# A planned order of 1300 steps, planned again with TensorE's instruction fetches and two corrected durations

## The chip, the cores and the metric

The kernel runs on one core of a Trainium2 chip. The metric is the device time of one execution in microseconds (us). All operands are float32 at the kernel's interface; the products are formed from two or three float32r (rounded float32) parts, so that the result has float32 accuracy.

## The reference, cut to what matters

Three layers follow each other on a batch of 2 with 768 positions: an attention with a local window and block summaries (8 heads of 64), a token-mixing layer with a rotation, and a gated layer with a second mixing of tokens.

```python
# attention: q, k, v (2, 8, 768, 64)
k_sum, v_sum = max and mean of k, v over blocks of 32 positions
scores = [scale*q@k.T where |i-j| < 16, else -1e9 ; scale*q@k_sum.T + log(32)]
x = softmax(scores) @ [v ; v_sum]                # heads joined: (2, 768, 512)
# token mixing
theta = x @ w_theta
y = w_tok_r @ (x*cos(theta)) + w_tok_i @ (x*sin(theta))
u = x + y
x = u + max(u @ w_ch, 0)
# gated layer
h = gelu(x @ w_in);  u, v = halves of h
v = layernorm(v) * g_ln;  v = w_sg @ v + b_sg
out = x + (u*v) @ w_out
```

## The kernel before, in words

**The steps.** The kernel function (L547) does not write instructions where they stand in the text. It calls `op(...)` (L391) some 1300 times. Each call names a step, the engines that may do it with an estimated duration on each, the steps that it comes after, the buffers that it takes, and, for a load, its size. Examples are `S` (L915: 52 small matmuls, the scores of one pair of heads and one half of the positions), `PT` (L944: three transposes), `O` (L960: 24 small matmuls with the values), `X` (L981: three transposes), `th` (L1019: three matmuls of 512 columns for theta), `y` (L1098: six matmuls of the token mixing), `ch`, `iv`, `iu` (twelve matmuls of 512 columns each), `Qp` (L1435: nine of 384 columns) and `o` (L1490: the output).

**The planner.** `Order.play` (L442) runs on the host while the program is built. It is a list scheduler: it keeps a time at which each engine is free, and again and again takes, among the steps that could start soonest, the one with the smallest key. A key is a due time. Due times come from `PLAN` (where a stage is meant to lie, L37), and are followed backwards through the graph with a lead for each kind of step (`LEAD`, L48) and an offset for each single step (`SHIFT`, L64 on). `SHIFT` has a second number for loads: it moves the earliest time at which a load may be issued. Where a step has two engines, `play` also picks the engine, by the estimated durations. The list that comes out, sorted by planned start, is then issued in this order (L1536). So the numbers in the three tables never reach the chip; what reaches it is the order of instructions on each engine, the engine of each step, the buffer of each tile, and the number of filler matmuls.

**Fillers.** Between planned times 6 and 36 us, `play` puts bfloat16 matmuls without use (L707) where it sees TensorE idle (L509 to L511); each counts 0.2025 us.

**Loads.** All transfers are issued by SP, at most 8 in flight by the plan (`OUT`, L379). The 57 MB that move include inputs, the weights, the output, and matrices that are put aside to DRAM and read back.

**The order in time.** Attention of both halves of the batch is mixed with theta and with the splitting of weights into a high and a low part, up to about 100 us. Then come `y`, `ch`, `iv` and `iu` to about 297 us, the second token mixing (`Qp`, tile `Qs`) and the output (`o`) to the end.

**What the changed lines touch.** The constants of class `Order` (L376 to L385), `play` (L442 to L543) at the place where a step gets its end (L513), the duration of `vo` on ScalarE (L1221, normalising one 128x512 block of v, either on ScalarE at L1215 or on VectorE at L1218), and the duration of `Qn` (L1378, the step at L1379 on VectorE).

Of the kernel before, what the change touches and what calls it, by code (L numbers as in the profile page):

```python
# [18 lines left out]
B, H, S, D = 2, 8, 768, 64  # L19
# [18 lines left out]
    q_from=121.281, q_step=28.693, q_back=223.53, at0=-10.9, at0_pair=7.346, at0_half=2.395,  # L38
    at1=30.092, at1_pair=3.285, at1_half=4.867, th0=27.719, th0_step=4.256, th1=34.789,
    th1_gap=17.348, th1_step=24.005, y00=98.094, y00_step=24.656, y01=63.431, y01_step=19.591,  # L40
    y10=147.759, y10_step=8.224, y11=160.878, y11_step=12.492, k_early=56.892, vt_early=1.56,
    q_early=4.908, v_early=-11.766, s_early=11.963, pt=-73.034, o=3.795, x=51.425, y_gap=3,
    w_spare=2, v_spare=1, z_spare=6, y_spare=0, q_spare=2, table=13.626, mode=5.473, bsg=250.456,
# [5 lines left out]
    Qz=74.168, ks=-40.136, vs=-11.881, vm=11.936, vr=-13.929, e=17.901, Pt=48.07, n=-10.669,  # L49
    xe=4.677, xh=9.148, xl=4.343, kk=-1.1, rr=-29.76, sc=-13.602, zm=-9.187, zh=7.556, zl=38.914,  # L50
    w_tht=8.728, w_rt=13.865, w_it=-1.048, w_rit=-8.999, k=-3.022, q=-3.059, v=1.199, vT=9.157,
    w_rd=22.528, w_id=-5.655, w_rid=3.014, w_thd=-9.579, bsg=-5.815, ch_e=13.7, d=14.634,
    gagf=-1.524, gh=8.649, gl=15.226, gm=-10.408, iu_g=88.574, iv_g=-16.768, m=-33.701,
    o_e=-19.883, rv=-3.588, sq=1.118, st=-55.633, tx=-19.318, tx_h=10.785, u=-3.396, u_h=-9.153,
    uv=-43.926, vh=6.864, vl=9.675, vo=-7.023, vp=0.039, w_chd=6.133, w_chh=-0.456, w_chl=3.459,
    w_chr=-13.975, w_cht=58.117, w_ih=-5.761, w_il=-46.919, w_inud=10.646, w_inuh=12.592,
    w_inul=-13.707, w_inur=8.343, w_inut=57.665, w_invd=15.806, w_invh=-50.158, w_invl=-21.398,
    w_invt=-8.855, w_ir=22.177, w_outd=-25.619, w_outh=15.605, w_outl=-21.45, w_outr=6.525,
    w_outt=12.079, w_rh=5.347, w_rih=6.258, w_ril=-15.3, w_rir=-13.172, w_rr=-12.082,
    w_sgd=9.125, w_sgh=5.251, w_sgl=6.738, w_sgsd=-2.394, w_sgsh=-4.109, w_sgsl=-4.009,  # L60
    w_thh=-3.486, ab=-11.929, o_ae=-17.964, o_be=5.444, w_invr=-3.314, w_rl=6.746, w_thl=8.414,
    w_thr=-2.869, Qaa=-36.615, Qab=18.479, Qac=-4.476, Qad=32.953, Qba=-7.182, Qbb=-4.881,
    Qbc=-45.244, Qbd=0.242, Qd=-14.617, Qe=15.488, Qg=4.768, Qh=-3.207, Qk=-11.256, Ql=5.491,
    Qm=10.937, Qu=-4.014, Qv=11.136, Qw=28.942, Qxh=5.023, Qxl=-5.36, gc=0.703, gt=2.997,  # L64
    gw=24.853, Qn=-29.771, Qx=-8.957, Qyh=1.69, Qyl=-22.283)
# [4 lines left out]
    warm0=(3.965, 0), masks0=(-3.862, 0), sets=(3.556, 0), masks2=(1.455, 0),  # L70
    cst=(15.845, 2.915), fill=(-9.642, 0), w_th0d=(-3.673, 15.198), w_th0t=(2.45, 0),
    w_th0r=(-.408, 0), w_th0h=(-1.22, 0), w_th0l=(.268, 0), w_th1d=(-1.914, -18.157),
    w_th1t=(1.029, 0), w_th1r=(-1.741, 0), w_th1h=(1.156, 0), w_th1l=(-.234, 0),
    w_th2d=(1.529, 5.971), w_th2t=(1.909, 0), w_th2r=(-1.914, 0), w_th2h=(-1.157, 0),
    w_th2l=(-.108, 0), w_th3d=(4.03, -1.082), w_th3t=(-2.527, 0), w_th3r=(-.575, 0),
    w_th3h=(-1.077, 0), w_th3l=(1.202, 0), w_r0d=(-.168, -2.081), w_r0t=(.588, 0),
    w_r0r=(-1.087, 0), w_r0h=(1.116, 0), w_r0l=(-1.655, 0), w_i0d=(-1.155, 15.003),
    w_i0t=(4.861, 0), w_i0r=(1.493, 0), w_i0h=(.108, 0), w_i0l=(-1.832, 0),
    w_ri0d=(3.082, -21.492), w_ri0t=(-7.525, 0), w_ri0r=(-.588, 0), w_ri0h=(-4.096, 0),
    w_ri0l=(-4.15, 0), w_r1d=(2.146, 10.79), w_r1t=(2.919, 0), w_r1r=(-1.704, 0),  # L80
    w_r1h=(-1.983, 0), w_r1l=(-1.058, 0), w_i1d=(-1.983, 11.44), w_i1t=(.641, 0),
    w_i1r=(4.405, 0), w_i1h=(-1.438, 0), w_i1l=(3.002, 0), w_ri1d=(.07, -2.92),
    w_ri1t=(-5.223, 0), w_ri1r=(.001, 0), w_ri1h=(-.079, 0), w_ri1l=(5.236, 0),
    w_r2d=(-7.111, -10.609), w_r2t=(.053, 0), w_r2r=(4.47, 0), w_r2h=(-5.26, 0),
    w_r2l=(-2.052, 0), w_i2d=(11.782, -14.445), w_i2t=(4.916, 0), w_i2r=(-.222, 0),
    w_i2h=(1.104, 0), w_i2l=(-1.867, 0), w_ri2d=(-1.883, 3.84), w_ri2t=(-.804, 0),
    w_ri2r=(-.544, 0), w_ri2h=(-5.231, 0), w_ri2l=(-2.723, 0), w_r3d=(-1.364, -8.117),
    w_r3t=(-3.117, 0), w_r3r=(4.499, 0), w_r3h=(-7.344, 0), w_r3l=(-5.466, 0),
    w_i3d=(7.147, 1.379), w_i3t=(-2.77, 0), w_i3r=(-5.827, 0), w_i3h=(-8.506, 0),
    w_i3l=(4.281, 0), w_ri3d=(-12.998, -22.098), w_ri3t=(1.16, 0), w_ri3r=(-2.26, 0),  # L90
    w_ri3h=(.737, 0), w_ri3l=(.496, 0), w_r4d=(6.596, -7.956), w_r4t=(-4.96, 0), w_r4r=(.092, 0),
    w_r4h=(.009, 0), w_r4l=(-10.529, 0), w_i4d=(-11.202, -6.738), w_i4t=(-1.817, 0),
    w_i4r=(-8.488, 0), w_i4h=(-1.595, 0), w_i4l=(.021, 0), w_ri4d=(6.591, -2.316),
    w_ri4t=(-.414, 0), w_ri4r=(1.569, 0), w_ri4h=(-3.272, 0), w_ri4l=(4.015, 0),
    w_r5d=(12.123, 3.875), w_r5t=(-2.799, 0), w_r5r=(.332, 0), w_r5h=(-.403, 0),
    w_r5l=(-12.426, 0), w_i5d=(8.685, 2.603), w_i5t=(2.874, 0), w_i5r=(-10.224, 0),
    w_i5h=(7.798, 0), w_i5l=(-2.331, 0), w_ri5d=(1.821, -1.805), w_ri5t=(-2.508, 0),
    w_ri5r=(6.718, 0), w_ri5h=(-.537, 0), w_ri5l=(3.889, 0), w_ch0d=(19.331, -7.138),
    w_ch0t=(6.055, 0), w_ch0r=(.748, 0), w_ch0h=(-3.195, 0), w_ch0l=(2.036, 0),
    w_inv0d=(9.499, -8.007), w_inv0t=(5.274, 0), w_inv0r=(.996, 0), w_inv0h=(4.98, 0),  # L100
    w_inv0l=(-2.049, 0), w_inu0d=(-13.818, -1.564), w_inu0t=(-1.458, 0), w_inu0r=(-2.338, 0),
    w_inu0h=(-.759, 0), w_inu0l=(-2.165, 0), w_out0d=(15.204, -.19), w_out0t=(-1.162, 0),
    w_out0r=(2.291, 0), w_out0h=(.433, 0), w_out0l=(-1.945, 0), w_ch1d=(16.728, -2.047),
    w_ch1t=(7.412, 0), w_ch1r=(2.329, 0), w_ch1h=(-5.061, 0), w_ch1l=(-2.158, 0),
    w_inv1d=(4.343, 25.037), w_inv1t=(4.333, 0), w_inv1r=(-4.484, 0), w_inv1h=(-6.68, 0),
    w_inv1l=(1.636, 0), w_inu1d=(.261, 7.019), w_inu1t=(-.294, 0), w_inu1r=(.089, 0),
    w_inu1h=(-.203, 0), w_inu1l=(-8.147, 0), w_out1d=(-.818, -12.348), w_out1t=(-9.747, 0),
    w_out1r=(8.904, 0), w_out1h=(1.734, 0), w_out1l=(-1.038, 0), w_ch2d=(.538, -2.903),
    w_ch2t=(1.69, 0), w_ch2r=(-7.301, 0), w_ch2h=(-6.013, 0), w_ch2l=(12.698, 0),
    w_inv2d=(-4.374, 3.585), w_inv2t=(2.573, 0), w_inv2r=(-10.543, 0), w_inv2h=(-2.155, 0),  # L110
    w_inv2l=(3.273, 0), w_inu2d=(1.469, -12.171), w_inu2t=(-7.233, 0), w_inu2r=(6.19, 0),
    w_inu2h=(.16, 0), w_inu2l=(3.335, 0), w_out2d=(-8.129, 13.059), w_out2t=(-2.468, 0),
    w_out2r=(1.649, 0), w_out2h=(1.94, 0), w_out2l=(8.626, 0), w_ch3d=(-10.817, .348),
    w_ch3t=(12.679, 0), w_ch3r=(-.467, 0), w_ch3h=(1.597, 0), w_ch3l=(-3.745, 0),
    w_inv3d=(4.498, 23.929), w_inv3t=(3.927, 0), w_inv3r=(-12.463, 0), w_inv3h=(-6.41, 0),
    w_inv3l=(-.612, 0), w_inu3d=(-33.946, 8.24), w_inu3t=(-11.179, 0), w_inu3r=(11.109, 0),
    w_inu3h=(-.226, 0), w_inu3l=(-3.959, 0), w_out3d=(3.083, -2.301), w_out3t=(-7.438, 0),
    w_out3r=(-9.562, 0), w_out3h=(-4.008, 0), w_out3l=(9.331, 0), bsg=(-1.132, -14.765),
    gsb=(-9.009, -4.653), k0=(-2.077, 2.465), vT0=(-1.406, 8.393), q0_0=(-2.902, -6.024),
    v0_0=(-5.683, -20.788), q0_1=(-1.661, -11.041), v0_1=(1.221, -13.607), ks0=(-1.935, 0),  # L120
    vs0=(-.384, 0), vp0=(-.982, 0), vm0=(1.331, 0), vr0_0=(.565, 0), vr0_1=(-.112, 0),
    M0_0=(.715, 0), L0_0=(16.171, 0), S0_0=(-.974, 0), m0_0=(1.748, 0), d0_0=(3.374, 0),
    e0_0=(-.864, 0), PT0_0_0=(.279, 0), Pt0_0_0=(-1.129, 0), PT0_0_1=(-.179, 0),
    Pt0_0_1=(-3.379, 0), O0_0=(-.69, 0), n0_0=(1.191, 0), X0_0=(2.894, 0), xe0_0=(-.971, 0),
    xh0_0=(.292, 0), xl0_0=(-.509, 0), S0_1=(-3.646, 0), m0_1=(2.69, 0), d0_1=(2.687, 0),
# [421 lines left out]
def kernel(  # L547
# [61 lines left out]
    def act(n):  # L609
        return 0.19 + 0.00084 * n  # L610
# [915 lines left out]
    t = 190  # L1526
# [73 lines left out]
```

## Time and profile before

| | us |
|---|---|
| median of 3 runs | 382.21 |
| lowest and highest | 379.33 and 382.38 |
| the profiled execution | 380.85 |
| its span, first to last instruction | 379.1 |
| TensorE busy in it | 369.4 |
| VectorE busy in it | 261.6 |
| ScalarE busy in it | 204.1 |
| GpSimd busy in it | 120.1 |

Outside the span lie 380.85 - 379.1 = 1.75 us. TensorE has two rows: PE for the matmuls, PEld for the loading of their stationary operand; each matmul has one of each. The ends of matmuls are modelled, so TensorE's busy time is an upper figure.

### The profile page before, as it was taken

To read this page: it belongs to the slowest core of one execution; us is meant where nothing else is said; L and a number is where in the kernel's file an instruction comes from. 1 tells how busy PE (TensorE), PEld (TensorE's weight loads), DVE (VectorE), ACT (ScalarE), POOL (GpSimd) and SP (SyncE) were. 2 spreads that over 40 slices of the span, in tenths; PEclk is the share of its full clock that TensorE was granted. 3 is DMA by queue.
4 is the path that set the end of the run, shared out by engine and by line. 5 is a ranking of instruction groups with operands and counts; after the bars stand their busy time and mean duration, and the time that the engine had idled before them with its cause. 6 is when DMAs were issued, how large, how long until landed. Compare 5 with 4: busy or idle time off the path is not lost.

```text
span 379.1 us, 7679 instructions
## 1 busy us (share of the span) xinstructions
PE 369.4 (97%) x2991; PEld 321.9 (85%) x2991; DVE 261.6 (69%) x453; ACT 204.1 (54%) x349; POOL 120.1 (32%) x145
## 2 busy tenths in 40 slices
PE   8898999999999999999999999999999999999996
PEld 4786888888888888888888788888888999999996
DVE  4997999999975964436674968684134487689621
ACT  2586699967874862234743862458234876332100
POOL 6663488553310200002620163335000046521000
PEclk9998999999999999999999999999999999999999
DMA  7999897992005041002556921646021443511222
GB/s 267 334 338 305 297 315 191 316 345 70 0 9 215 2 145 62 2 0 80 182 171 240 355 99 64 228 158 218 0 83 43 125 144 106 158 52 58 91 103 84
DMA packets 27332, 57.38 MB, mean 151 GB/s; under 512 B 3424, under 2 KB 16800, under 8 KB 27296
## 3 DMA queue, kind: packets, MB, share of 16 engines
q1 hardware_dynamic: 27296, 56.90, 44.9%
q8 instruction: 23, 0.38, 0.4%
q14 instruction: 13, 0.11, 0.1%
HBM read 45.18 MB, written 11.40 MB: 149 GB/s over the span
## 4 chain that ended last, share of the span: by engine, by line
PE 82%; DMA 5%; DVE 5%; ACT 3%; issue 2%; POOL 1%; SPq 1%; POOLq 0%; DVEq 0%; ACTq 0%
PE y L650 6%; PE y L651 6%; PE y L652 6%; PE Qs L650 3%; PE Qs L651 3%; PE Qs L652 3%; PE ch L650 3%; PE ys L651 3%; PE ch L651 3%; PE ys L652 3%; PE iu L652 3%; PE iu L651 3%; PE ch L652 3%; PE iu L650 3%; PE iv L652 3%; PE iv L651 3%
## 5 line engine op out<-in xcount | busy, mean ns | idle before, releaser
L645 DVE TENSOR_TENSOR z<-f,z 128x512 fp32r<-128x512 f32 x21 | 14.9, 709 | 20.8 <-ACT z L637 20.6
L650 PE MATMUL Qs<-Qx,Qh 128*128 128x384 f32 x84 | 28.2, 336 | 0.2 <-DVE U L1458 0.2
L652 PE MATMUL Qs<-Qx,Ql 128*128 128x384 f32 x84 | 28.1, 334 | 0.0
L651 PE MATMUL Qs<-Qx,Qh 128*128 128x384 f32 x84 | 28.1, 334 | 0.0
L652 PE MATMUL ys<-w_ri,z 128*128 128x256 f32 x96 | 27.1, 282 | 0.0
L651 PE MATMUL ys<-w_ri,z 128*128 128x256 f32 x96 | 27.1, 282 | 0.0
L650 PE MATMUL ys<-w_ri,z 128*128 128x256 f32 x96 | 26.7, 278 | 0.0
L637 ACT ACTIVATE z<-f 128x512 fp32r<-128x512 f32 x19 | 11.9, 627 | 23.7 <-PE ys L652 18.1
L650 PEld LDWEIGHTS ys<-w_ri,z 128*128 128x128 f32 x96 | 18.0, 188 | 4.4
L637 ACT ACTIVATE Qx<-Qx 128x768 fp32r<-128x768 f32 x20 | 16.6, 843 | 9.3 <-DMA Qx<-dQx 6.4
L651 PEld LDWEIGHTS ys<-w_ri,z 128*128 128x128 f32 x96 | 18.0, 188 | 3.8
L650 PE MATMUL th<-w_th,xh 128*128 128x512 f32 x48 | 20.6, 428 | 0.2 <-DVE xT L642 0.2
L1061 DVE TENSOR_TENSOR f<-f,x 128x512 f32<-128x512 f32 x21 | 16.0, 763 | 5.4 <-ACT f L1055 5.1
L652 PE MATMUL th<-w_th,xh 128*128 128x512 f32 x48 | 19.3, 402 | 0.3 <-DVE xh L645 0.3
L650 PE MATMUL y<-w_i,z 128*128 128x512 f32 x48 | 19.3, 402 | 0.0
L651 PE MATMUL th<-w_th,xh 128*128 128x512 f32 x48 | 19.3, 401 | 0.0
L650 PE MATMUL y<-w_r,z 128*128 128x512 f32 x48 | 19.2, 399 | 0.0
L651 PE MATMUL y<-w_r,z 128*128 128x512 f32 x48 | 19.0, 397 | 0.0
L651 PE MATMUL y<-w_i,z 128*128 128x512 f32 x48 | 19.0, 395 | 0.0
L645 DVE TENSOR_TENSOR Ql<-vx,Qh 128x768 fp32r<-128x768 f32 x10 | 9.4, 960 | 13.7 <-PE iu L652 9.4
L650 PE MATMUL ch<-u,w_ch 128*128 128x512 f32 x48 | 18.8, 392 | 0.0
L650 PE MATMUL iu<-tx,w_inu 128*128 128x512 f32 x48 | 18.7, 390 | 0.0
(357 smaller groups left out, 1174.2 us busy)
## 6 DMA issues: line engine op xcount, KB each, us to landing
Qx<-dQx SPq DMA_DIRECT2D x21, 384.0 KB, 3.7
v<-in_vW_dram SPq DMA_DIRECT2D x16, 193.5 KB, 5.1
k<-in_kT_dram SPq DMA_DIRECT2D x8, 384.0 KB, 6.5
q<-in_qT_dram SPq DMA_DIRECT2D x16, 192.0 KB, 5.0
vT<-in_vT_dram SPq DMA_DIRECT2D x8, 384.0 KB, 5.2
w_r<-in_w_rT_dram SPq DMA_DIRECT2D x6, 511.8 KB, 5.0
w_i<-in_w_iT_dram SPq DMA_DIRECT2D x6, 511.8 KB, 5.6
Qw<-in_w_sgT_dram SPq DMA_DIRECT2D x12, 192.0 KB, 2.5
```

The costliest lines, as they stand in the source:

```text
L637: ACT.activation(dst, src, AF.Copy, scale=scale)
L645: EN[e].tensor_tensor(out=lo, in0=src, in1=hi.bitcast(F32), op=ALU.subtract)
L650: PE.matmul(ps, ah, bh, start=first, stop=False, skip_group_check=True)
L651: PE.matmul(ps, ah, bl, start=False, stop=False, skip_group_check=True)
L652: PE.matmul(ps, al, bh, start=False, stop=last, skip_group_check=True)
L1061: EN[e].tensor_tensor(out=z3(), in0=z3(), in1=x.unsqueeze(1).to_broadcast([P, 2, 256]), op=ALU.mult)
```

## The change

The planner learns of a second thing that TensorE can wait for: its own instructions. A new method `fetch` counts TensorE's instructions along the planned list. After 246 instructions, and every 256 from there, a block of 256 is asked for; it is there 3.3 us later (or 3.3 us after the block before it), and TensorE may not pass instruction 446 (and every 256 from there) until the block is there. What a step is late by is added to its end. `CODE` says how many instructions each kind of step has; a kind that it does not list has 24.

```diff
     FILL = 0.2025
+    FETCH = 3.3
+    BLOCK, ASK, HAVE = 256, 246, 446
+    CODE = {"M": 10, "L": 48, "S": 104, "O": 48, "PT": 6, "X": 6, "th": 6, "y": 12, "vp": 2, "Qp": 18,
+            "fill": 10}
...
+    def fetch(self, n, d, s):
+
+        late, at, end = 0.0, self.at, self.at + n
+        while True:
+            ask = self.ASK + self.BLOCK * len(self.come)
+            have = self.HAVE + self.BLOCK * self.had
+            if ask <= have:
+                if ask >= end:
+                    break
+                t = s + late + max(0, ask - at) * d / n
+                self.come.append(max(t, self.come[-1] if self.come else 0.0) + self.FETCH)
+            else:
+                if have >= end:
+                    break
+                t = s + late + max(0, have - at) * d / n
+                late += max(0.0, self.come[self.had] - t)
+                self.had += 1
+        self.at = end
+        return late
...
     def play(self):
         self.link()
+        self.at, self.had, self.come = 0, 0, []
...
             f = s + o.eng[e]
+            if e == "PE":
+                if n > 0 and self.FILL_FROM < s < self.FILL_TO:
+                    self.fetch(2 * n, n * self.FILL, free_at["PE"])
+                code = "".join(c for c in o.name if not c.isdigit()).strip("_")
+                f += self.fetch(self.CODE.get(code, 24), o.eng[e], s)
             free_at[e] = f - self.OVER[e]
...
-            op(f"vo{b}_{i}", {"ACT": act(512), "DVE": 0.54}, norm, after=[f"rv{b}"], use=[vx],
+            op(f"vo{b}_{i}", {"ACT": 0.8, "DVE": 0.54}, norm, after=[f"rv{b}"], use=[vx],
...
-                op("Qn" + tag, {"DVE": dve(384)},
+                op("Qn" + tag, {"DVE": 0.61},
```

`act(512)` is 0.62 us and `dve(384)` is 0.553 us. No instruction of any step is changed. The tables are all new: every entry of `PLAN` that is a time, nearly all of `LEAD`, and 1286 of the 1299 entries of `SHIFT` (the mean move of a due time's offset is 2.3 us, the largest 27.5 us). Of `PLAN`:

```diff
-    q_from=121.281, q_step=28.693, q_back=223.53, at0=-10.9, at0_pair=7.346, at0_half=2.395,
-    at1=30.092, at1_pair=3.285, at1_half=4.867, th0=27.719, th0_step=4.256, th1=34.789,
-    th1_gap=17.348, th1_step=24.005, y00=98.094, y00_step=24.656, y01=63.431, y01_step=19.591,
-    y10=147.759, y10_step=8.224, y11=160.878, y11_step=12.492, k_early=56.892, vt_early=1.56,
...
+    q_from=104.904, q_step=25.508, q_back=237.29, at0=-14.501, at0_pair=7.571, at0_half=1.496,
+    at1=29.474, at1_pair=3.67, at1_half=5.605, th0=26.39, th0_step=6.327, th1=25.273,
+    th1_gap=37.416, th1_step=27.103, y00=109.705, y00_step=26.181, y01=59.749, y01_step=27.551,
+    y10=164.594, y10_step=16.055, y11=158.349, y11_step=14.503, k_early=51.523, vt_early=-1.525,
...
```

The pace of the first half's attention (`at0_pair`, one pair of heads each 7.3 to 7.6 us) hardly moves; the second half's theta is spread (`th1_gap` 17.3 to 37.4), the token mixing of the first half is due 11.6 us later in its first part (`y00`), and the last matrices may be loaded earlier (`q_from` 121 to 105) and read back later (`q_back` 224 to 237).

## Rows read from the trace of the kernel before

**Rows 1.** The page: span, busy time, TensorE's granted clock, DMA share, instruction queue, one group.

```profile
span 379.1 us, 7679 instructions
...
PE 369.4 (97%) x2991; PEld 321.9 (85%) x2991; DVE 261.6 (69%) x453; ACT 204.1 (54%) x349; POOL 120.1 (32%) x145
...
PEclk9998999999999999999999999999999999999999
DMA  7999897992005041002556921646021443511222
...
q8 instruction: 23, 0.38, 0.4%
...
L651 PE MATMUL th<-w_th,xh 128*128 128x512 f32 x48 | 19.3, 401 | 0.0
```

**Rows 2.** Stretches: busy us of each engine (instructions), granted clock, DMA share.

```profile
0.00:10.00 10.00, 8.21 (x121) 4.53 (x122) 4.51 (x6) 2.45 (x3) 6.57 (x23) 1.00 0.81 273
10.00:20.00 10.00, 8.68 (x230) 7.44 (x230) 9.30 (x17) 6.18 (x11) 6.99 (x13) 1.00 1.04 332
20.00:30.00 10.00, 9.45 (x232) 8.36 (x230) 9.73 (x21) 8.93 (x18) 5.71 (x8) 1.00 1.03 331
30.00:40.00 10.00, 8.28 (x108) 6.88 (x105) 6.91 (x14) 6.94 (x13) 4.07 (x4) 0.83 0.92 301
40.00:100.00 60.00, 59.15 (x864) 49.38 (x863) 57.61 (x102) 49.85 (x83) 34.32 (x39) 1.00 0.71 233
100.00:300.00 200.00, 200.00 (x1008) 170.11 (x1007) 122.86 (x204) 103.90 (x186) 43.41 (x44) 1.00 0.34 115
300.00:310.00 10.00, 9.78 (x57) 9.46 (x56) 6.60 (x9) 7.66 (x12) 3.26 (x2) 1.00 0.34 124
```

**Rows 3.** Waits of TensorE over the span: us in total, times, longest.

```profile
PE S L890 <- issue: 1.7, 1, 1.7
PE S L881 <- DVE P L929: 1.3, 4, 0.4
PE warmb L703 <- DVE warm L690: 1.3, 1, 1.3
PE PT L942 <- ACT P L937: 0.6, 1, 0.6
```

**Rows 4.** Timeline of TensorE, 0 to 40 us: start, length, line, tiles, idle before.

```profile
6.19 2.00 PE L710 MATMUL fill_B<-maskb,identb 128*128 128x480 bf16 x9
...
30.10 0.32 PE L881 MATMUL S<-maskb,identb 64*64 64x288 bf16 x4
30.25 0.50 PE L890 MATMUL S<-k,q 64*64 64x96 f32 x14
32.46 0.41 PE L890 MATMUL S<-k,q 64*64 64x96 f32 x9 [1.72 <-issue]
...
34.79 0.63 PE L651 MATMUL th<-w_th,xh 128*128 128x512 f32 x1
```

**Rows 5.** Stretches from the start: instructions of PE, then PEld, begun by then.

```profile
0.00:25.85 25.85, 22.74 (x479) 17.07 (x480) 19.49 (x34) 13.46 (x24) 16.37 (x40) 1.00 0.95 308
0.00:30.10 30.10, 26.44 (x578) 20.36 (x578) 23.64 (x42) 17.66 (x31) 19.27 (x43) 1.00 0.96 313
...
0.00:32.40 32.40, 27.08 (x596) 20.82 (x597) 25.65 (x44) 19.84 (x34) 21.17 (x45) 1.00 0.97 311
```

**Rows 6.** DMA queues, 30.06 to 31.2 us: packets, MB, share of 16 engines.

```profile
q1 hardware_dynamic: 115, 0.32, 98.3%
q8 instruction: 1, 0.02, 6.1%
```

**Rows 7.** Lines L1215, L1218 and L1379: durations in ns (least/median/most).

```profile
L1215 ACT ACTIVATE vx<-vx,rs x8: 798/804/807, 258.8 to 302.0; 128x512 f32<-128x512 f32 x8
...
L1218 DVE TENSOR_SCALAR vx<-vx,mv,rs x4: 541/802/1327, 256.9 to 296.6; 128x512 f32<-128x512 f32 x4
...
L1379 DVE SCALAR_TENSOR_TENSOR R<-R,g_sb,bsg x8: 605/608/612, 328.2 to 345.0; 128x384 f32<-128x384 f32 x8
```

More of the change, by code (lines that the diff above doesn't have):

```diff
@@ L37 @@
 PLAN = dict(
-    q_from=121.281, q_step=28.693, q_back=223.53, at0=-10.9, at0_pair=7.346, at0_half=2.395,
-    at1=30.092, at1_pair=3.285, at1_half=4.867, th0=27.719, th0_step=4.256, th1=34.789,
-    th1_gap=17.348, th1_step=24.005, y00=98.094, y00_step=24.656, y01=63.431, y01_step=19.591,
-    y10=147.759, y10_step=8.224, y11=160.878, y11_step=12.492, k_early=56.892, vt_early=1.56,
-    q_early=4.908, v_early=-11.766, s_early=11.963, pt=-73.034, o=3.795, x=51.425, y_gap=3,
-    w_spare=2, v_spare=1, z_spare=6, y_spare=0, q_spare=2, table=13.626, mode=5.473, bsg=250.456,
+    q_from=104.904, q_step=25.508, q_back=237.29, at0=-14.501, at0_pair=7.571, at0_half=1.496,
@@ L44 @@
+    at1=29.474, at1_pair=3.67, at1_half=5.605, th0=26.39, th0_step=6.327, th1=25.273,
+    th1_gap=37.416, th1_step=27.103, y00=109.705, y00_step=26.181, y01=59.749, y01_step=27.551,
+    y10=164.594, y10_step=16.055, y11=158.349, y11_step=14.503, k_early=51.523, vt_early=-1.525,
+    q_early=5.493, v_early=-12.787, s_early=9.634, pt=-87.98, o=1.46, x=51.512, y_gap=3,
+    w_spare=2, v_spare=1, z_spare=6, y_spare=0, q_spare=2, table=7.737, mode=7.289, bsg=229.532,
     far0=6, far1=8, trees=109)
@@ L48 @@
 LEAD = dict(
[L49 to L60, printed above, removed]
@@ new lines @@
+    Qz=87.604, ks=-44.861, vs=-11.04, vm=12.223, vr=-12.804, e=26.99, Pt=35.168, n=-24.726,
+    xe=-12.95, xh=17.944, xl=10.168, kk=-6.961, rr=-16.126, sc=-14.493, zm=-14.357, zh=15.348,
+    zl=52.975, w_tht=5.595, w_rt=18.363, w_it=13.589, w_rit=-15.295, k=-4.387, q=-0.015,
+    v=-1.513, vT=9.276, w_rd=22.472, w_id=-11.472, w_rid=-12.412, w_thd=-11.034, bsg=-12.167,
+    ch_e=19.977, d=16.589, gagf=-1.524, gh=8.649, gl=15.226, gm=-10.408, iu_g=91.746,
+    iv_g=-13.124, m=-37.993, o_e=-47.73, rv=-21.122, sq=16.069, st=-60.102, tx=-33.635,
@@ new lines @@
+    tx_h=5.101, u=3.381, u_h=-11.178, uv=-40.914, vh=6.864, vl=9.675, vo=-5.156, vp=0.701,
+    w_chd=6.725, w_chh=4.788, w_chl=17.211, w_chr=-24.862, w_cht=59.307, w_ih=-15.279,
+    w_il=-52.513, w_inud=28.92, w_inuh=9.098, w_inul=-15.25, w_inur=-1.948, w_inut=50.141,
+    w_invd=27.073, w_invh=-39.83, w_invl=-7.418, w_invt=-4.457, w_ir=29.298, w_outd=-33.593,
+    w_outh=28.413, w_outl=-25.579, w_outr=23.976, w_outt=1.779, w_rh=2.336, w_rih=5.558,
+    w_ril=-1.178, w_rir=-32.455, w_rr=-9.115, w_sgd=9.125, w_sgh=5.251, w_sgl=6.738,
```

603 lines of the change are left out of this document (303 added, 300 removed).

## The prediction

> **What bounds the kernel now.** I read the page first: TensorE is busy 369.4 of 379.1 us, and its clock is granted in full but for one slice, the fourth; the DMA engines are full in the first tenth and half empty later [rows 1]. So nearly all of the time is matmuls that this change doesn't touch, and only TensorE's gaps can be won. The stretches say where these are. From 100 to 300 us TensorE is busy 200.00 of 200 us, from 300 to 310 us 9.78 of 10. Before 100 us the gaps are 1.79, 1.32, 0.55, 1.72 and, from 40 to 100, 0.85 us, 6.2 us in all, and in the stretch from 30 to 40 us the clock is 0.83 on the mean [rows 2]. The waits name them: the longest is 1.7 us before a score matmul at L890, ended by nothing that the profile shows ("issue"); then 1.3 us in four waits for VectorE at L929, and 1.3 us for the first memset [rows 3].
>
> The timeline shows the longest one closely. The 52 matmuls of a step `S` begin at 30.10, stop after eighteen, and go on at 32.46 in the middle of the step, where no other engine's result is needed. Theta's matmuls behind it show 0.63 us [rows 4] against 0.40 on the mean of all 48 [rows 1]: the engine was starved for 1.72 us and then ran slow. The mean clock of 0.83 over 10 us is 1.7 us of TensorE's work lost, at 1.2 instead of 2.4 GHz for some 3.4 us [rows 2]. While it stood, one packet of the instruction queue went by among 115 others, with the 16 DMA engines 98.3% full of data [rows 6]. In the whole span that queue has 23 packets and 0.38 MB, one for some 260 of TensorE's 5982 instructions [rows 1]. So the wait is for TensorE's next block of instructions, and that block was late behind the loads.
>
> VectorE matters beside it: 9.30 and 9.73 of 10 us from 10 to 30, 57.61 of 60 from 40 to 100, but only 6.91 in the stretch of the stall [rows 2]. What TensorE wins there must also be won by VectorE, which does a part of every step of the attention.
>
> **The fetches in the plan.** This part issues nothing. It works only through the order, so its worth is the stall, if the new order is free of it. I try the planner's constants on the old order at the trace's pace. The planner counts 104 instructions for the first `S`, which has 48 (its other parts are `M` and `L`), so its count is 56 ahead. The fourth block is asked for at its 1014, that is at 958 true ones: at 25.85 us 479 + 480 had begun. It must be there at 1214, 1158 true ones: 578 + 578 at 30.10. With 3.3 us the block is there at 29.15, 0.95 us before it is needed: no stall by the planner's rule. On the chip TensorE stopped at 596 + 597 instructions and went on at 32.46, 6.6 us after the asking [rows 4, 5]. So the place of the stop agrees within 40 instructions, but the delay is twice the planner's where the loads fill the DMA engines. The planner may avoid a stall in its own plan and still leave one on the chip; equally, any new order shifts which step meets the block's end and how full the queues are then. I hold it somewhat likelier than not that it goes: three earlier blocks passed in an equally full stretch (DMA share 1.04 and 1.03) and no other wait of the engine is put down to "issue" [rows 2, 3].
>
> What the stall is worth: on TensorE 1.72 us of standing plus 1.7 us of lost clock, 3.4 us. But VectorE did 6.91 us there against 9.73 us in the stretch before, 2.8 us less, and it has only 2.4 us of slack in the 60 us that follow [rows 2]. I take the smaller, 2.8 us; the larger holds if VectorE's work can be moved past 100 us, where it is busy 122.86 of 200. What is late next is VectorE itself, or another block by a little: 0.4 us, one more wait like the longest on L929 [rows 3], given back.
>
> At this place the Trainium skill's page "Runtime: NRT & Kernel Launch", section "Instruction fetch mechanics", says that blocks of 256 instructions (16 KiB) are fetched ahead by the engine's own queue, and that this is hidden because the sequencer issues more slowly than the fetch fills. The trace agrees with the size of the block (0.38 MB in 23 packets) and not with the hiding: a stop of 1.72 us in the middle of a step. By that rule there would be no fetch to wait for and the change would be worth nothing, 380.85 us; it is the third rival below.
>
> **Two durations.** `vo` on ScalarE took 804 ns eight times out of eight, the plan had 0.62; `Qn` took 608 ns, the plan had 0.553 [rows 7]. 12 `Qn` by 0.055 is 0.7 us of VectorE that the plan did not know of; no work on the chip is made longer. The first can move a `vo` to VectorE, which takes 541 ns at the least but 802 at the median of four [rows 7]: a gain of 0.26 us or nothing. All of it lies beside matmuls: TensorE misses 0.22 us in the stretch from 300 to 310, where the last `vo` stand [rows 2]. Bounds: 0.22 us gained, and 0.4 us lost if one such step lands on the path; I take 0.
>
> **All other moves.** The matmuls are the same, so beyond 100 us nothing can be won but that 0.22 us, and a loss needs a step that starves TensorE for the first time. VectorE is 61% busy from 100 to 300 and ScalarE 52%, DMA 0.34 [rows 2]: later due times for `y`, earlier loads of the last matrices and later read-backs have cover, and without it cost some tenths each, as the waits do now. The loads that are moved pass through SP's one queue; their price is on the fetches (above) and on the loads that attention waits for, in the 30 us where the DMA share is 0.8 to 1.04. Before 100 us the other gaps (6.2 - 1.72 = 4.5 us) and the fillers between 6.19 and 8.19 (2.0 us that stand for idle time [rows 4]) are at most 6.5 us, of which 1.3 us is the start. The slack of VectorE says that little of the rest can go; I take 0, with a bound of 2 us gained and 2 us lost.
>
> **The sum.** 380.85 - 2.8 + 0.4 = 378.45, say 378.5 us, against the profiled execution; the median of the runs is 382.21, 1.4 us higher, and the runs span 3.05 us. A measurement of this kernel tells 1% from no change, 3.8 us, hardly less; the forecast is 0.97% under the median, so it lies on that edge.
>
> **The rivals.**
>
> *The stall stays or moves* (0.25). For it: 3.3 us against 6.6 measured, and the pace of the first attention is kept, so the same density of instructions meets the same full DMA engines. Against it: one block of the first four was late, not all. The time is 380.85 us less a few tenths, 380.5.
>
> *Two blocks late, slower than before* (0.12). The planner takes 3.3 us for safe, and may pack two `S` close to a block's end where it kept them apart by chance; or loads issued earlier put more data ahead of the block. Each late block costs 1.7 us, and the second one a clock drop of its own, 1.7 us: 380.85 + 3.4 = 384.3 us. It decides when a second block is needed less than 6.6 us after it is asked for while the DMA share is 1.0. For it: the old order had only 4.25 us (25.85 to 30.10) between asking and need [rows 5]. Against it: of 23 blocks one has stopped the engine visibly [rows 1, 3].
>
> *It was no fetch* (0.06). Then the order is only another one, and the stop finds its place again: 380.85 us. Against it speaks the packet [rows 6].
>
> *More is won* (0.14). The new order also takes 2 us of the start, out of fillers and waits: 376.5 us. For it: 4.5 us of other gaps. Against it: VectorE's slack.
>
> **How the numbers follow.** The forecast has 0.43, the rivals 0.25, 0.12, 0.06 and 0.14. The range leaves out the case of two late blocks and what lies past the best one: 375.5 (the best case less 1) to 382.5 (the case of a stall that stays, plus 2 for moves that lose). Faster by over 1% takes under 378.4: nearly half of the forecast's own cases, all of the best, a little of the first rival: 0.38. Slower by over 1% takes over 386.0 against the median or 384.7 against the profiled one: most of the slow rival: 0.10. The rest, 0.52, is no difference.
>
> **What would show it.** Right: no wait of TensorE on "issue" above 0.5 us before 100 us, the granted clock full in every slice of the first 100 us, VectorE above 9 us in each 10 from 20 to 100, TensorE's busy time down by some 2 us (the slow matmuls gone), no new gap past 100 us. Wrong: a stop in the middle of an `S` or `O` again, with an instruction packet in it; a second drop of the clock; waits of TensorE for DMA'd operands in the first 60 us; or a gap past 100 us, which would mean that the new due times starve the token mixing.

## The result and the profile after

The new order is slower by a little. Twenty executions of it have a median of 382.12 us (379.99 to 385.62), twenty of the kernel before 380.15 (378.47 to 382.38): a ratio of 1.0057, with an interval of 1.0037 to 1.0077. The loss of 0.57% is below the 1% that the prediction's chances ask about, but its interval lies clear of no change, and the forecast was a gain of 0.97%. Of the twenty executions of the new kernel eighteen had lost clock (mean granted clock under 0.998); the two that had not took 380.66 and 379.99 us. The profiled execution of the new kernel took 382.25 us against 380.85.

The page of the kernel after, the rows that answer to [rows 1]:

```profile
span 380.5 us, 7678 instructions
...
PE 369.5 (97%) x2993; PEld 321.6 (85%) x2993; DVE 265.5 (70%) x461; ACT 202.4 (53%) x349; POOL 109.1 (29%) x133
...
PEclk9999999999999999999999899999999999999999
DMA  8999987971004221004577803646021334310322
...
q8 instruction: 23, 0.38, 0.4%
```

The slice with the lower clock has moved from the fourth (28 to 38 us) to the twenty-third (209 to 219 us). The stretches of the kernel after, as in [rows 2], with one of ten us added:

```profile
0.00:10.00 10.00, 8.54 (x125) 4.48 (x126) 4.86 (x6) 3.18 (x5) 6.56 (x23) 1.00 0.85 287
10.00:20.00 10.00, 7.94 (x223) 6.92 (x221) 9.11 (x16) 5.66 (x10) 7.33 (x14) 1.00 1.01 322
20.00:30.00 10.00, 9.10 (x212) 8.04 (x212) 9.16 (x19) 8.00 (x15) 5.33 (x7) 1.00 0.99 332
30.00:40.00 10.00, 9.56 (x171) 7.77 (x174) 9.35 (x18) 9.18 (x18) 4.09 (x4) 1.00 0.97 322
40.00:100.00 60.00, 59.78 (x844) 50.09 (x837) 56.42 (x98) 52.09 (x88) 31.41 (x34) 1.00 0.69 228
100.00:300.00 200.00, 197.04 (x983) 167.00 (x982) 123.69 (x213) 98.30 (x177) 38.58 (x37) 0.99 0.34 112
210.00:220.00 10.00, 7.04 (x25) 5.40 (x24) 6.45 (x11) 8.25 (x13) 0.62 (x1) 0.84 0.75 293
300.00:310.00 10.00, 10.00 (x59) 10.00 (x58) 5.71 (x7) 6.54 (x11) 2.77 (x2) 1.00 0.53 185
```

Before 100 us TensorE's gaps are 1.46, 2.06, 0.90, 0.44 and 0.22 us, 5.1 in all against 6.2, and the clock is full where it was 0.83 [rows 2], which cost 1.7 us: 2.8 us gained. From 100 to 300 us, where the kernel before had no gap, 3.0 us are missing, all between 210 and 220, and there a mean clock of 0.84 takes 1.6 us more: 4.6 us lost. From 300 to 310 us 0.22 is won. The sum, -2.8 + 4.6 - 0.2 = +1.6, stands for the 1.4 us by which the spans differ. The waits of TensorE of the kernel after name the places:

```profile
PE ch L683 <- ACT ut L1269: 3.0, 1, 3.0
PE warmb L736 <- DVE warm L723: 1.3, 1, 1.3
PE S L914 <- DVE P L962: 1.2, 3, 0.4
PE S L923 <- issue: 1.1, 1, 1.1
```

The old stall of 1.7 us on "issue" has become 1.1 us [rows 3]; the first row is new. Both are in the timeline of TensorE of the kernel after (start, length, line, tiles, idle before):

```profile
18.64 0.52 PE L923 MATMUL S<-ks,q 64*64 64x24 f32 x22
20.23 0.29 PE L923 MATMUL S<-ks,q 64*64 64x24 f32 x2 [1.07 <-issue]
...
213.08 0.39 PE L685 MATMUL iu<-tx,w_inu 128*128 128x512 f32 x1
216.43 0.50 PE L683 MATMUL ch<-u,w_ch 128*128 128x512 f32 x1 [2.96 <-ACT ut L1269]
216.76 0.59 PE L684 MATMUL ch<-u,w_ch 128*128 128x512 f32 x1
217.15 0.63 PE L685 MATMUL ch<-u,w_ch 128*128 128x512 f32 x1
```

The stop at 19 us is again in the middle of an `S`; no drop of the clock followed it here. The one at 213.5 us is not a fetch: `ch` waits for the PSUM bank that ScalarE's gelu has to empty, and then its matmuls of 512 columns run at 0.63 us instead of 0.39. What held the gelu stands in the timeline of ScalarE of the kernel after (the tile that the trace calls `zero` is a staging buffer of the step `w_inv…t`):

```profile
205.91 0.80 ACT L793 ACTIVATE zero<-w_inv 128x512 f16<-128x512 bf16 x1 [1.43 <-DMA w_inv<-in_w_in_dram]
210.57 0.78 ACT L793 ACTIVATE zero<-w_inv 128x512 f16<-128x512 bf16 x1 [3.86 <-DMA w_inv<-in_w_in_dram]
211.23 1.65 ACT L670 ACTIVATE u<-xT 128x512 fp32r<-128x512 f32 x3
212.78 0.78 ACT L793 ACTIVATE zero<-w_inv 128x512 f16<-128x512 bf16 x1
214.49 1.28 ACT L1269 ACT_TABLE_LOAD   x1 [0.93 <-DMA dQx<-Qy16h]
215.78 0.60 ACT L1269 ACTIVATE ut<-iu 128x512 f32<-128x512 f32 x1
```

Two things stand ahead of the gelu (with its load of the function table). ScalarE does its steps in the order of its list and is held 3.86 us, up to 210.57, by a step that waits for a weight of 512 KB. And the gelu's output tile `ut0_0` got the buffer H16, out of which `Qy16h` is being stored to DRAM; the store has to end first. The DMA issues of the kernel after, 200 to 216 us (count, KB each, us from issue to landing):

```profile
w_out<-in_w_out_dram SPq DMA_DIRECT2D x4, 511.8 KB, 7.8
w_inv<-in_w_in_dram SPq DMA_DIRECT2D x3, 511.8 KB, 6.7
...
dQx<-Qy16h SPq DMA_DIRECT2D x1, 192.0 KB, 9.2
```

The store of 192 KB took 9.2 us because SP had issued four loads of 512 KB from 202.5 us on, ahead of it. In the order before, `ut0_0` had a buffer (H8) that no store had to empty, and the table load followed ScalarE's last copy at once. The timeline of ScalarE of the kernel before:

```profile
212.75 1.16 ACT L637 ACTIVATE u<-xT 128x512 fp32r<-128x512 f32 x2 [0.48 <-DVE xT L1109]
213.93 1.28 ACT L1236 ACT_TABLE_LOAD   x1
```

### The profile page after: what moved, and what is told of

Its sections match the earlier page's. It is cut to its first block, busy times and chain, and to the rows that moved or that the text cites. A ratio compares the mean times of both kernels' runs of the same rounds, so it can differ in the third digit from the quotient of the medians.

```text
span 380.5 us, 7678 instructions
## 1 busy us (share of the span) xinstructions
PE 369.5 (97%) x2993; PEld 321.6 (85%) x2993; DVE 265.5 (70%) x461; ACT 202.4 (53%) x349; POOL 109.1 (29%) x133
## 4 chain that ended last, share of the span: by engine, by line
PE 91%; DMA 3%; DVE 3%; ACT 2%; issue 1%; DVEq 0%
PE y L683 6%; PE y L684 6%; PE y L685 6%; PE Qs L685 4%; PE Qs L684 4%; PE Qs L683 4%; PE th L683 3%; PE ch L683 3%; PE ch L685 3%; PE ch L684 3%; PE ys L685 3%; PE ys L684 3%; PE ys L683 3%; PE iv L685 3%; PE iv L684 3%; PE iv L683 3%
## 5 line engine op out<-in xcount | busy, mean ns | idle before, releaser
L678 DVE TENSOR_TENSOR z<-f,z 128x512 fp32r<-128x512 f32 x21 | 17.4, 829 | 15.5 <-ACT z L670 14.8
L670 ACT ACTIVATE Qx<-Qx 128x768 fp32r<-128x768 f32 x21 | 17.4, 845 | 10.2 <-PE Qs L685 4.7
L683 PE MATMUL ch<-u,w_ch 128*128 128x512 f32 x48 | 19.3, 403 | 3.0 <-ACT ut L1269 3.0
L670 ACT ACTIVATE z<-f 128x512 fp32r<-128x512 f32 x17 | 10.8, 633 | 19.6 <-PE ys L685 12.4
L683 PE MATMUL th<-w_th,xh 128*128 128x512 f32 x48 | 20.1, 418 | 0.0
L685 PE MATMUL ch<-u,w_ch 128*128 128x512 f32 x48 | 19.4, 404 | 0.0
L684 PE MATMUL ch<-u,w_ch 128*128 128x512 f32 x48 | 19.4, 403 | 0.0
L1224 DVE BATCH_NORM_STATS2 st<-vx 128x6 f32<-128x512 f32 x12 | 8.3, 688 | 15.9 <-ACT vx L1214 15.9
L684 PE MATMUL th<-w_th,xh 128*128 128x512 f32 x48 | 18.9, 394 | 0.1
```

The lines of the kernel that those rows point to most:

```text
L670: ACT.activation(dst, src, AF.Copy, scale=scale)
L678: EN[e].tensor_tensor(out=lo, in0=src, in1=hi.bitcast(F32), op=ALU.subtract)
L683: PE.matmul(ps, ah, bh, start=first, stop=False, skip_group_check=True)
L684: PE.matmul(ps, ah, bl, start=False, stop=False, skip_group_check=True)
L685: PE.matmul(ps, al, bh, start=False, stop=last, skip_group_check=True)
L1224: DVE.bn_stats(out=st, in_=vf())
```

## The experiments

The theory: the change lost its time at this gelu, through two waits that end within 1 us of each other (ScalarE's last step on a weight ends at 213.56, the wait for the store at 214.49): the loads in ScalarE's order, and the store. What the change won before 100 us would then still be there. The rivals: that one of the two alone is the cause; that the loss comes from the planner's new code or the new durations; and that the front, not this place, decides the median.

**The buffer alone.** `other_buffer` takes the kernel after and exchanges the names of two buffers for all tiles planned after 208.7 us, so that `ut0_0` doesn't stand behind the store:

```diff
...
+    for o in plan:
+        for b, _ in o.new:
+            if o.start > 208.7 and order.where[b] in ("H7", "H16"):
+                order.where[b] = {"H7": "H16", "H16": "H7"}[order.where[b]]
...
```

> One edit to the kernel after: the tile ut0_0, which the first gelu of the block iu0 writes, changes places with the tiles that use buffer H7 from then on, so that it no longer waits for the store that empties buffer H16. Theory (two waits stand one behind the other on ScalarE: the landing of the load of w_inv3 at 210.55 us, and the landing of the store of Qy16h at 214.40; both feed the wait of 3.0 us of TensorE at 213.4): only the second is taken away, ScalarE's table load starts at 213.56 instead of 214.49, TensorE waits 2.0 us instead of 3.0 and its clock still drops; about 381.2 us where the kernel after has 382.1. Rival (the buffer alone is to blame): the wait of TensorE goes below 0.5 us, about 378.0 us. Second rival (the load alone): nothing changes, 382.1 us.

Median 382.12 us (378.85 to 386.79, 10 runs), ratio 1.005 (1.0016 to 1.0084). The median is no better than the kernel after's, where 381.2 was expected, though the interval holds that time too. The profile is of an execution at full clock (379.32 us); its timeline of ScalarE:

```profile
210.14 0.79 ACT L793 ACTIVATE zero<-w_inv 128x512 f16<-128x512 bf16 x1 [3.31 <-DMA w_inv<-in_w_in_dram]
...
213.15 1.28 ACT L1269 ACT_TABLE_LOAD   x1
```

The table load no longer waits for the store and comes 1.3 us earlier, but ScalarE still stands for the weight, and `ch` waits 1.7 us. Two of the ten executions ran at full clock, 379.32 and 378.85 us, some 1.2 us under the two of the kernel after that did. The other eight lost clock; no profile shows where, so that this takes back what the shorter wait gave is not shown.

**ScalarE's order alone.** `act_order` keeps the buffers and puts three steps on the weights behind the gelu, two of ScalarE and the VectorE step that follows the first (`behind` moves steps in the planned list):

```diff
...
+    behind(["w_inv3t", "w_inv0t", "w_inv3r"], "iu0_0g")
```

> One edit to the kernel after: on ScalarE the two steps that wait for the loads of w_inv3 and w_inv0, and the VectorE step behind the first of them, stand behind the first gelu of iu0 instead of ahead of it; buffers as before. Theory (two waits one behind the other): the copies of u move up to 209 us, but the gelu still waits for the store of Qy16h that empties its buffer, to 214.4 us; TensorE's wait stays at 2.5 to 3.0 us, 381.6 to 382.1 us. Rival (the load alone is to blame): the wait goes below 0.5 us, about 378.0 us.

Median 382.66 us (380.92 to 385.06, 10 runs), ratio 1.0071 (1.0038 to 1.0104). The waits of TensorE:

```profile
PE ch L683 <- ACT ut L1269: 3.2, 1, 3.2
...
PE S L923 <- issue: 2.0, 1, 2.0
```

The timeline of ScalarE, the DMA issues from 200 to 216 us, and the stretch of 210 to 225 us:

```profile
217.39 1.28 ACT L1269 ACT_TABLE_LOAD   x1 [4.45 <-DMA dQx<-Qy16h]
```

```profile
dQx<-Qy16h SPq DMA_DIRECT2D x1, 192.0 KB, 9.4
```

```profile
210.00:225.00 15.00, 11.81 (x53) 9.23 (x51) 9.26 (x17) 8.93 (x15) 1.90 (x2) 1.00 0.64 229
```

With the loads out of ScalarE's way the wait is as long as before: the store alone is enough to hold the gelu. That the load alone is the cause is excluded. In this execution the clock stayed full after the wait at `ch`; it had fallen at 23 us, behind the stop of 2.0 us that ended at 21.8.

**Both.** `buffer_and_order` has the two edits together.

> Both edits at once: the gelu's other buffer and the later place of the steps that wait for w_inv3 and w_inv0. Theory: TensorE's wait at 213 us falls to 0.7 us or less, its clock is granted in full from 6 us on, and the 2.3 us of lead that the kernel after has over the kernel before between 90 and 210 us stays to the end: 377.5 to 379.0 us, faster than the kernel before (380.15) by about 2 us. Rival (the lead is lost in any case, since VectorE or the loads are what is late past 210 us): a wait of 2 us or more appears elsewhere between 205 and 235 us, and the time is 380 us or more.

Median 379.63 us (378.24 to 381.82, 12 runs), ratio to the kernel before 0.9984 (0.996 to 1.0008). The waits of TensorE:

```profile
PE S L923 <- issue: 1.3, 2, 0.8
...
PE ch L683 <- DVE xT L1188: 0.4, 1, 0.4
```

The wait for ScalarE is gone and 2.5 us with it (382.12 to 379.63), and all twelve executions had a mean clock of 0.999 or more. Neither edit alone moved the median, both together did: two waits of nearly the same end, one hidden behind the other. The time lies 0.6 us above the top of what was expected, and the interval does not exclude the time of the kernel before.

**The store brought forward.** `stores_first` has the buffers of the kernel after, ScalarE's new order, and two of the loads issued behind the stores on SP:

```diff
...
+    behind(["w_inv3t", "w_inv0t", "w_inv3r"], "iu0_0g")
+    behind(["w_inv0d", "w_out1d"], "Qz17")
```

> Buffers as in the kernel after, ScalarE's order as in the run with the changed order, and on SP the loads of w_inv0 and w_out1 stand behind the stores of Qy16 and Qy17 instead of ahead of them. Theory (the store of Qy16h took 9.2 us because 512 KB loads were in front of it in the same queues): without two of these four loads it lands about 3 us earlier, at 211 to 212 us, the gelu starts by 213 us, and TensorE's wait is below 0.7 us: 377.5 to 379.0 us. Rival (the store is slow by itself, a write to DRAM beside reads): it still takes 8 us or more and the wait stays at 2.5 us or more, about 382 us.

Median 379.17 us (377.57 to 381.32, 10 runs), ratio 0.9977 (0.9949 to 1.0004). The DMA issues, 200 to 216 us:

```profile
w_inv<-in_w_in_dram SPq DMA_DIRECT2D x3, 511.8 KB, 3.7
...
dQx<-Qy16h SPq DMA_DIRECT2D x1, 192.0 KB, 3.7
```

The timeline of ScalarE:

```profile
208.25 1.76 ACT L670 ACTIVATE u<-xT 128x512 fp32r<-128x512 f32 x3 [1.79 <-DVE xT L1142]
210.60 1.28 ACT L1269 ACT_TABLE_LOAD   x1 [0.59 <-issue]
211.90 0.60 ACT L1269 ACTIVATE ut<-iu 128x512 f32<-128x512 f32 x1
```

The same store from the same buffer lands after 3.7 us instead of 9.2, and the gelu starts 3.9 us earlier, with the shared buffer still there. From `act_order` it differs by the place of these two loads alone: 9.4 us to landing there, 3.7 here. So it is the place of the store behind the loads that made the buffer late, not the sharing as such. The same kernel once more (`stores_first_again`):

> The run with the stores first once more, with more rounds, since three repaired kernels gave 0.9977, 0.9984 and 1.0001 of the kernel before. Theory (the front of the new order is worth about 1 us, as the medians of the profiles' fronts say): ratio 0.996 to 0.999, no wait of TensorE above 0.5 us between 100 and 300 us. Rival (the front is worth nothing, since its blocks of instructions come late as in the old order): ratio 0.999 to 1.001.

Median 378.98 us (377.87 to 380.62, 12 runs) against 380.02 for the kernel before: 0.9977 (0.9958 to 0.9997). It is the one version whose interval lies clear of the kernel before, by 0.23%; it is 3.1 us under the kernel after at the medians. Its interval overlaps those of the other repaired kernels, so that it is better than they are is not shown. A wait of 0.6 us of `ch` for VectorE remained, a little more than was expected.

**All three edits.** `all_three` adds the buffer exchange to `stores_first`.

> The kernel after with the other buffer for the first gelu, ScalarE's two weight steps behind it, and the loads of w_inv0 and w_out1 behind the stores. Theory (each of the last two runs left one wait of a few tenths): no wait of TensorE between 100 and 300 us above 0.3 us; 378.5 to 379.3 us at the median, 0.2 to 0.4% under the kernel before. What is left of its spread is the stops at TensorE instruction 705 and 1217. Rival (the front of the new order is worth no more than the old one's): within 0.1% of the kernel before, 379.8 to 380.4.

Median 379.26 us (377.99 to 382.94, 12 runs), ratio 1.0001 (0.9976 to 1.0026). The medians are 379.26 and, for the kernel before beside it, 379.79; the ratio is that of the rival, no difference. No gain over `stores_first` is measured; the wait of 0.6 us for VectorE is here too, against what was expected. Once the store lands early, the buffer is free early, and exchanging it is worth nothing that can be measured.

**The code without the tables, the tables without the code.** `code_alone` has the new planner and durations with the tables of before (`PLAN`, `LEAD`, `SHIFT`); `tables_alone` has the new tables with the planner and durations of before. Of the edit of `tables_alone`:

```diff
-    FETCH = 3.3
...
-                f += self.fetch(self.CODE.get(code, 24), o.eng[e], s)
...
-            op(f"vo{b}_{i}", {"ACT": 0.8, "DVE": 0.54}, norm, after=[f"rv{b}"], use=[vx],
+            op(f"vo{b}_{i}", {"ACT": act(512), "DVE": 0.54}, norm, after=[f"rv{b}"], use=[vx],
...
```

> The tables of the kernel before with the planner's new code: the fetches and the two durations, without the new order's tables. TensorE's steps then stand in the same order as in the kernel before in the first 276 of 315, SP's in all; what differs are engines and buffers of steps past 245 us. Theory (the change lives in the tables alone; the new terms of the planner move nothing before 245 us): as the kernel before within 0.5%, 379.0 to 381.5 us, with the stop of TensorE at its block's end near 30 us in some executions. Rival (the fetches in the planner change the front of the order): no such stop, and 378 us or less.

> The tables of the kernel after with the planner's old code. TensorE's order is that of the kernel after in all 315 steps, SP's but for two. Theory: as the kernel after, 381.5 to 383 us, TensorE waits 2 to 3 us for the first gelu at 213 us. Rival (the new terms of the planner are what keeps or costs the time): 380 us or less, or 384 or more.

`code_alone`: median 379.7 us (379.03 to 381.05, 10 runs), ratio 0.9994 (0.9972 to 1.0015). TensorE's steps come in the same order up to the 276th of 315. `tables_alone`: median 383.25 us (381.62 to 384.42, 4 runs), ratio 1.0091 (1.0061 to 1.012). Its waits of TensorE:

```profile
PE ch L653 <- ACT ut L1239: 3.8, 1, 3.8
...
PE S L893 <- issue: 1.1, 1, 1.1
```

The loss comes with the tables, with the same wait at the same place; the counting of fetches and the two durations do nothing by themselves that can be measured.

**The fault put into the kernel before.** `before_shared_buffer` exchanges two buffers there so that `ut0_0` comes to stand behind the store of `Qy13h`; nothing else is touched.

```diff
...
+            if o.start > 206.5 and order.where[b] in ("H0", "H8"):
+                order.where[b] = {"H0": "H8", "H8": "H0"}[order.where[b]]
...
```

> The kernel before with the fault of the kernel after put into it: from 206.5 us on by the plan, buffers H0 and H8 change places, so that the first gelu's tile takes the buffer that a store (Qy13, issued at 211.5 us, both parts landed by 219.4) must empty first. Nothing else is moved. Theory (a store behind 512 KB loads holds the gelu, the gelu holds the bank that ch needs): TensorE waits 3 to 5 us near 216 us, its clock drops, 383.5 to 387 us. Rival (a free bank is found, or VectorE and the loads are what is late there in any case): under 1 us more, 380 to 381 us.

Median 386.97 us (386.56 to 387.65, 4 runs), ratio 1.0193 (1.0171 to 1.0216). The waits of TensorE, then the timeline of ScalarE:

```profile
PE ch L650 <- ACT ut L1236: 5.7, 1, 5.7
```

```profile
217.79 1.28 ACT L1236 ACT_TABLE_LOAD   x1 [5.85 <-DMA dQx<-Qy13h]
```

Two names exchanged cost the kernel before some 7 us: 5.7 of waiting, and the clock fell at 218 us. All four executions lost clock.

**The stops on "issue".** There are fourteen profiled executions: of the kernels before and after, and of the experiments. In thirteen of them TensorE has a pause of over 0.5 us on "issue" before 50 us, in one of these it has two. I counted its instructions in the records (matmuls, weight loads and the sequencer's own) up to each of the fourteen pauses: all stand behind instruction 446 + 256k + 3, that is 705, 961 or 1217. They last 0.72 to 2.5 us from start to start, in the old and the new order alike (1.96 us in the kernel before, at 1217; 1.28 in the kernel after, at 705). Two more pauses stand at 705, in `code_alone` (1.15 us) and `before_shared_buffer` (0.75), where the profile names a result of ScalarE as what came last. The one kernel without such a pause is the next.

The instruction queue tells what they wait for. Its transfers are of 16 KB; the second one belongs to 705, the third to 961, the fourth to 1217. By the records each of the sixteen pauses ends 1.27 to 1.57 us after the end of its own transfer, and in none of the fourteen executions does TensorE pass any of its first four blocks' ends less than 1.27 us after that. In the kernel before the fourth transfer runs from 30.07 to 31.18 us [rows 6] and TensorE goes on at 32.46.

`gates` is `stores_first` with 13 reads of 2 KB on SP, each of which waits for an earlier load, so that fewer loads are in flight from 13 to 30 us. The reads are extra work.

```diff
+    def gate(before, on):
...
+        g.fn = lambda e: nc.sync.dma_start(far[:], T(on)[:32, :n])
+        plan.insert([o.name for o in plan].index(before), g)
+    for before, on in (("q3_1", "k3"), ("vT3", "v1_0"), ("v2_0", "v1_1"), ("w_th0d", "q3_1"),
...
```

> The kernel of the run with the stores first, and between 13 and 30 us thirteen reads of 2 KB on SP, each of a tile whose load was issued four or five transfers before; a read can't be issued before that load has landed, so fewer loads are in flight. Theory (TensorE's blocks of instructions come late because they stand behind the loads in flight): the second block's transfer begins before 17 us instead of 17.8, the fourth's before 29; the stops of TensorE in the middle of a step near 19 and 31 us fall below 0.3 us, and the time falls by 0.5 to 1 us against the run with the stores first, to 378.2 to 378.7 us, faster than the kernel before. Rival (the delay of a block does not hang on the loads): stops of 0.7 to 2 us as before, 379.2 us or, if the loads themselves come too late, more.

Median 381.98 us (380.84 to 382.86, 12 runs), ratio 1.0045 (1.0021 to 1.0069). The waits of TensorE, then the stretches:

```profile
PE S L923 <- DMA q<-in_qT_dram: 1.3, 1, 1.3
```

```profile
10.00:20.00 10.00, 8.64 (x230) 7.63 (x230) 9.30 (x17) 5.81 (x10) 6.89 (x13) 1.00 0.81 260
20.00:30.00 10.00, 8.30 (x203) 7.01 (x202) 8.95 (x19) 7.35 (x14) 4.32 (x6) 1.00 0.89 258
```

With the DMA share at 0.81 and 0.89 instead of 1.01 and 0.99, the one profiled execution has no wait on "issue" of 0.2 us or more before 50 us (at 1217 it stands 0.34 us from start to start), and the clock was full in all 12 executions. But 260 and 258 GB/s instead of 322 and 332 go with later loads: now `S` waits 1.3 us for `q`, and the kernel is 2.8 us slower than without the gates, where a gain was expected. The blocks did not come sooner as expected either: the second transfer began at 17.11 us (16.06 and 17.82 in the two profiles without gates), the fourth at 30.21 (29.00 and 29.47). At 1217 it is TensorE that came later (32.4 us; 31.4 in `stores_first`). So that fewer loads in flight bring a block sooner is not shown.

`split_fillers` is `stores_first` with each filler matmul of 480 columns cut in two of 240: 11 fillers, 22 instructions more, so that a block's end meets an earlier step.

```diff
-            PE.matmul(ps[:, :5 * WK], identb[:], maskb[:].rearrange("p k c -> p (k c)"), start=True, stop=True)
+            for c in range(2):
+                half = maskb[:].rearrange("p k c -> p (k c)")[:, 240 * c:240 * c + 240]
+                PE.matmul(ps[:, :240], identb[:], half, start=True, stop=True)
```

> The kernel of the run with the stores first, with each of the 11 filler matmuls of 480 columns near 6 to 9 us split into two of 240: 22 more instructions on TensorE ahead of the stop, the same work. Theory (the stop is the end of what has been fetched): the stop near 19 us comes at the same count of instructions, so 11 matmuls earlier in the program: after 11 of the 24 short score matmuls of its step, where five runs showed it after 22. Rival (the stop belongs to the step or to its data): after 22 again, or none.

One execution, 377.7 us. The stop at 19 us is absent, so its shift could not be seen. Another is there, in the timeline of TensorE:

```profile
24.89 0.65 PE L977 MATMUL PT<-ident,P 128*120 128x128 f32 x4 [1.33 <-issue]
```

It stands at instruction 961 = 446 + 2 · 256 + 3. The place by count holds, and the third transfer had ended 1.31 us before; which of the blocks is late varies from execution to execution.

**The kernel before once more.** `before_again`, one execution:

> The kernel before once more, to see how much of what its one profile showed belongs to one execution. Theory (the stop at the block's end is there in each execution, its length varies with the loads, and the clock's drop behind it only comes with a long one): a stop of 0.3 to 1.5 us at TensorE instruction 449 + 256 k before 35 us, granted clock of 1.0 in that stretch, span 377 to 379 us. Rival (the profile was typical): 1.7 us and a drop of the clock near 33 us again, 379 us.

382.51 us, above what was expected. The waits of TensorE:

```profile
PE S L890 <- issue: 2.3, 1, 2.3
```

The stop at 1217 lasted 2.5 us from start to start this time, and the clock fell twice, at 11.6 and 35.5 us. With the old order's first 100 us the same stop has thus lasted 1.96, 0.85 (`code_alone`), 1.12 (`before_shared_buffer`) and 2.5 us: a profile of one execution doesn't tell its price.

## Why the prediction was wrong, point by point

**The step that failed** is "All other moves": "I take 0, with a bound of 2 us gained and 2 us lost", because VectorE at 61%, ScalarE at 52% and the DMA share of 0.34 from 100 to 300 us "have cover". The runs showed 3.0 us of waiting and 1.6 us of clock in the profile, past the bound, and 3.1 us at the medians (382.12 against the 378.98 of `stores_first_again`). The mean over 200 us was the wrong view to rest this on. In the ten us where it counted the DMA share was 0.75 at 293 GB/s, and the wait is not one for a busy engine: it comes from an engine that stands in order before a load, and from a buffer that is reused behind a store. Neither shows in a busy share. The prediction's last part had named the sign ("a gap past 100 us") but gave it no chance of its own; its only price was the bound of 2 us. That 382.12 lies inside the range, 375.5 to 382.5, is owed to this bound, added on top of a stall that stays: a case that the forecast did not take. The rival that was to end slower, two late blocks, was about the wrong place.

**The stall, -2.8 + 0.4.** The direction was right: in the profiles the kernel after is 2.8 us ahead by gaps and clock at 100 us. A second measure is the start of the 200th matmul of `y`. In the eight profiled executions with the new first 100 us, their loads as planned, and no drop of the clock there, it lies at 164.8 to 165.8 us, 165.4 on the mean; with the old one at 166.2 (`before_shared_buffer`) and 167.2 (`code_alone`) without a drop, at 168.0 and 169.9 (the kernel before, twice) with one. So the new order is worth 1.3 us at that place where no clock is lost and 3.5 us against an old execution that lost some. But the new order can lose it too: in `act_order`, whose clock fell at 23 us, the start is at 168.4. The size was taken from one execution that had lost clock: of 92 timed executions of the kernel before that ran beside the experiments, 57 had none of it (mean granted clock 0.998 or more; median 379.42 us) and 35 had (380.78). The repaired kernels, which keep the new first 100 us, are 0.45 (`buffer_and_order`), 0.53 (`all_three`) and 1.04 us (`stores_first_again`) under the kernel before at the medians, not 2.4. The median of 382.21 that the prediction started from was of three runs; that of twenty is 380.15.

**Why the stop stays.** The rival "the stall stays or moves" was right in its own terms: 1.1 us, from instruction 1217 to 705. Of the planner's constants the 446 and 256 are right: they stand in all fourteen stops, three instructions on, once the sequencer's own instructions are counted (24 by 1217), which the prediction left out. Its 246 is not: from 102 us on, blocks' transfers begin when 152 to 178 instructions of the 256 have begun, and in the first 50 us at 234 to 440. So the 6.6 us of the prediction, counted from 246, is not the delay of the block; that 3.3 us from there is too short holds (5.1 us, from 15.1 to 20.2, for the block at 705 in the kernel after). "It was no fetch" falls: the stops sit at the blocks' ends, and each ends 1.27 to 1.57 us after its block's transfer. That the block was late *behind the loads* stays likely and not shown. The Trainium skill's page "Runtime: NRT & Kernel Launch", section "Instruction fetch mechanics", has the fetch hidden behind the sequencer's issue; the runs here agree with its block of 256 instructions. They agree with the hiding at most blocks, and not at the one or two, of some 23, where TensorE stopped in thirteen of the fourteen profiles.

**Two durations, 0.** As predicted, as far as it can be told: `code_alone`, which has them, is at 0.9994 of the kernel before, and the 0.22 us in the stretch from 300 to 310 was won in the kernel after.

**The signs named.** VectorE above 9 us in each ten from 20 to 100: nearly right (9.16, 9.35, 56.42 of 60; 8.98 and 8.84 in the two tens from 70 to 90). Full clock in the first 100 us: right in the profiled execution, wrong in that of `act_order`. No "issue" above 0.5 us: wrong (1.1). TensorE's busy time down by 2 us: wrong (369.5 against 369.4), the slow matmuls being those of `ch` instead of theta's. No gap past 100 us: wrong, and this decided.

**What stays open.** Why one stop is followed by a drop of the clock and another of like length is not: 1.27 us idle at 10 us in `before_again` was, 1.57 us at 32 us in `other_buffer` was not; 2.96 us at `ch` in the kernel after was, 3.19 us at `ch` in `act_order` was not. What delays a block of instructions was not isolated. Not tried was a planner that knows of the buffer's store and of queued transfers.

## What to carry to other kernels

When an order is made anew, look at each buffer that is written again while its old content is still being stored: the wait here followed from the loads issued ahead of the store (9.2 or 3.7 us for the same 192 KB). Where two waits end at nearly the same time, remove both in one experiment before dropping either as a cause. Don't price a stall and the clock that follows it from one profiled execution; count first how many executions have it.

## What the runs showed of the hardware

- A store of 192 KB landed 9.2 us after its issue behind four loads of 512 KB (9.4 in `act_order`), and 3.7 us after it with two of these loads issued behind it (`stores_first`).
- TensorE stopped for 0.7 to 2.5 us at instruction 705, 961 or 1217 of its stream in thirteen profiled executions (DMA share 0.98 to 1.04 from 10 to 30 us), and for 0.34 us in that of `gates` (0.85). Each of the longer stops ended 1.27 to 1.57 us after a transfer of 16 KB on the instruction queue.
- A pause of 3 us of TensorE at full load was followed by half the clock for 3.4 us: 2.96 us idle, then matmuls of 512 columns that start 0.43 us apart up to 220.1 us, and 0.23 from there. After a pause of 1.07 us at 19 us in the same execution the clock stayed full, and so it did after 3.19 us at the same matmul in `act_order`.
